# Moving the value-cache loads of a decode-attention kernel from SyncE's DMA queue to ScalarE's

## The chip, the cores and the metric

The kernel runs on one core of one Trainium2 chip. The metric is the device time of one execution in microseconds (us), median of several executions. The profile's span, also quoted, is of one execution and comes out about 2 us shorter. "Tile" always means one unit of the kernel's main loop: one batch row and four heads, with 4 MB of keys, called K(t), and 4 MB of values, V(t); t runs from 0 to 63.

## The reference, cut to what matters

```python
def reference(A_x, A_k_cache, A_v_cache, A_wq, A_wo, B_x, B_w1, B_b1, B_w2, B_b2):
    # 8 batch rows, one query each; 32 heads; 4096 cached positions; head size 128; bf16
    x = A_x
    xn = _layernorm(x, axis=-1)
    # attention: q = xn @ wq; scores = q . k_cache * Dh**-0.5; p = softmax; o = p @ v_cache; o @ wo
    # mlp: gelu(layernorm(xn) @ w1 + b1) @ w2 + b2
    return x + _A_ref(xn, A_k_cache, A_v_cache, A_wq, A_wo) + _B_ref(xn, B_w1, B_b1, B_w2, B_b2)
```

Each cached key and value is used once. The two caches are 537 MB of the 552 MB that are read.

## The kernel before

The program is a list of operations. Each has an engine and a position; every engine runs its operations in order of position, and a small scheduler derives the semaphore waits from the tiles that an operation reads and writes. There are two buffers for keys (`NK = 2`) and two for values (`NV = 2`). All large loads are issued by SyncE ("sp"), in order, on one DMA queue:

```python
def ld(pos, dst, src, W, sem, R=()):
    add("sp", pos, lambda e: e.dma_start(dst, src() if callable(src) else src), R=R, W=W, sem=sem)
...
for t in range(T):                                       # T = 64 tiles
    pos = (-100.0, -98.0)[t] if t < NK else t - 1.5      # K(t): needs K(t-2)'s buffer
    for n, (j0, j1) in enumerate(kpieces(t)):
        ld(pos + 0.01 * n, kview(t)[:, j0:j1, :], ...)
    pos = (0.45, 1.2)[t] if t < NV else t + 0.6          # V(t): needs V(t-2)'s buffer
    for n, (j0, j1) in enumerate(vpieces(t)):            # one piece; V(63) in three
        ld(pos + 0.01 * n, vview(t)[:, j0:j1, :], ...)
...
for hg in range(NG - 1):                                 # output weights, once per 8 tiles, 640 KB
    ld(hg * B + 3.65, wo_sb[:, :, :], ...)
```

So from K(4) on, SyncE issues K(4), V(2), K(5), V(3), ... : K(t+2), then V(t). The work on a tile is this (the line numbers are those of the profile):

- VectorE multiplies three quarters of the keys by the query and sums, in two halves (L549 multiply, L553 add, L556 reduce). It holds the key buffer until the second multiply ends.
- TensorE transposes the other quarter, the first of the tile (L517), ScalarE evicts it, and TensorE multiplies it with the query (L527).
- For two tiles at a time (the last two one by one), the softmax: VectorE's row maximum (L568), transposes on TensorE (L570, L578), ScalarE's exponentials (L588).
- TensorE multiplies the probabilities with the values (L621; L631 for the last piece), about two tiles later: the value product of tile t stands in TensorE's order after the key work of tile t+2. ScalarE evicts it (L640).
- At the end a few multiplications by zero (L784) stand between the last products; they are meant to keep TensorE's clock up.

Of the kernel before, what the change touches and what calls it, by code (L numbers as in the profile page):

```python
# [19 lines left out]
class _Sched:  # L20
# [13 lines left out]
    def add(self, eng, pos, fn, R=(), W=(), X=(), sem=None, sig=False):  # L34
        o = _Op()
        o.pos, o.seq, o.eng, o.fn, o.R, o.W, o.X, o.sem = pos, len(self.ops), eng, fn, R, W, X, sem
        o.sig = sig
        self.ops.append(o)
# [165 lines left out]
def bass_parallel_sum__gqa_block_cached__mixer_channel_mlp__decode_kernel(  # L204
# [16 lines left out]
    HT = 4  # L221
# [3 lines left out]
    T = NG * B  # L225
# [12 lines left out]
    NK, NV, NS = 2, 2, 4  # L238
# [6 lines left out]
    with ExitStack() as es:  # L245
# [6 lines left out]
        wo_sb = sb("wo_sb", [P, HT, D], BF)  # L252
# [65 lines left out]
        add = sch.add  # L318
        TRR = _Ring("TR", 2)

        def kview(t):
            return KV_sb[:, t % NK, :].rearrange("p (j d) -> p j d", d=P)

        def vview(t):
            return KV_sb[:, NK + t % NV, :].rearrange("p (j d) -> p j d", d=P)
# [5 lines left out]
        def tile_src(cache, t):  # L331
            return cache[t % B, span(t // B, HT)].rearrange("h k d -> (h k) d").rearrange("(p j) d -> p j d", p=P)
# [19 lines left out]
        def dve_const2(e):  # L352
# [9 lines left out]
            W=["identneg", "onesb", "sel", "oTn", "wo"] + [(s, i) for s in ("Pt", "rs") for i in range(GT)])  # L362


        def ld(pos, dst, src, W, sem, R=()):
            add("sp", pos, lambda e: e.dma_start(dst, src() if callable(src) else src), R=R, W=W, sem=sem)  # L366

        add("act", -100, lambda e: e.dma_start(x_sb[:, :], x2[:, :]), W=["x"], sem="x")
        add("act", -99.9, lambda e: e.dma_start(b2_sb[:, :], B_b2.partition_broadcast(B)), W=["b2"], sem="b2")
        add("act", -99.8, lambda e: e.dma_start(b1_sb, B_b1.rearrange("(o f) -> o f", o=1)), W=["b1"], sem="b1")  # L370

        ld(-99.0, wq_sb, A_wq.rearrange("(k c) n -> k c n", c=DC), ["wq"], "wq")

        def pvpos(i):
            return 2.0 + i

        def kpieces(t):
            return [(0, NJ)]

        def vpieces(t):  # L380
            return [(0, 64), (64, 96), (96, NJ)] if t == T - 1 else [(0, NJ)]

        for t in range(T):
            pos = (-100.0, -98.0)[t] if t < NK else t - 1.5
            for n, (j0, j1) in enumerate(kpieces(t)):
                ld(pos + 0.01 * n, kview(t)[:, j0:j1, :], lambda t=t, j0=j0, j1=j1: tile_src(A_k_cache, t)[:, j0:j1, :],
                   [("K", t % NK, q) for q in range(j0 // 16, j1 // 16)], "k%d_%d" % (t % NK, n))
            pos = (0.45, 1.2)[t] if t < NV else t + 0.6
            R = (["wqfree"], ["wqfree", "w1free", "hfree"])[t] if t < NV else []
            for n, (j0, j1) in enumerate(vpieces(t)):  # L390
                ld(pos + 0.01 * n, vview(t)[:, j0:j1, :], lambda t=t, j0=j0, j1=j1: tile_src(A_v_cache, t)[:, j0:j1, :],
                   [("V", t % NV, q) for q in range(j0 // 16, j1 // 16)], "v%d_%d" % (t % NV, n), R)
        ld(-95.2, w1_sb, B_w1.rearrange("(k c) f -> k c f", c=DC), ["w1"], "w1")
        ld(-95.1, w2_sb[:, 0:FC, :], B_w2[0:FC * P, :].rearrange("(k c) n -> k c n", c=FC), ["w2"], "w2")
        ld(-95.0, w2_sb[0:FR, FC, :], B_w2[FC * P:F, :], ["w2r"], "w2r")
# [3 lines left out]
               "wo")  # L399

        wo_last = A_wo[(H - HT) * P:H * P, :].rearrange("(a p) n -> p a n", p=P)
        ld(T - 0.1, wo_sb[:, 0:HT - 1, :], wo_last[:, 0:HT - 1, :], ["wo"], "wo")
        ld(T - 0.09, wo_sb[:, HT - 1, :], wo_last[:, HT - 1, :], ["wo3"], "wo3")


        def layernorm(n, pos, src, src_res, dst, dst_res):
# [21 lines left out]
        def transposed(w, pos, src, src_res):  # L428
# [16 lines left out]
            R=["x", "b2"], W=["xb2"])  # L445
# [254 lines left out]
        def pe_zero(e):  # L700
# [6 lines left out]
            R=["zeros"], W=["ACC"], X=["ACC"])  # L707
# [14 lines left out]
        def pe_hidden(e):  # L722
# [10 lines left out]
            R=[it_h], W=["h"], X=[it_h])  # L733

        def pe_hidden_t(e):
# [7 lines left out]
            R=[it_t], W=["hT"], X=[it_t])  # L743

        def pe_mlp2(e):
# [11 lines left out]
            R=["mlp", "xb2"], W=["xb2"], X=[("PVb", 0), ("PVb", 1)])  # L757
# [6 lines left out]
            R=["ACC"], W=["resT"], X=["ACC"])  # L764
# [21 lines left out]
        for pos, n in ((pvpos(T - 2) + 0.25, 2), (pvpos(T - 1) + 0.075, 4), (pvpos(T - 1) + 0.115, 3), (pvpos(T - 1) + 0.2, 1)):  # L786
# [3 lines left out]
            R=["fin"], W=["out0"], X=[("TR", 0)])  # L790
        add("act", END + 2, lambda e: e.activation(out_sb[:, w:D], TRF[32:32 + B, 0, 0:w], ACT.Copy),
            R=["fin"], W=["out1"], X=[("TR", 0, "act")])
# [51 lines left out]
```

## Time and profile before

| | |
|---|---|
| time | 1290.62 us, median of 3 (1290.62 to 1290.68) |
| span of the profiled execution | 1288.9 us |
| DMA engines busy | 99.9% with one queue |
| VectorE busy | 87% |
| TensorE busy, ScalarE busy | 50%, 39% |

The page's list of engines, its rows by slice for VectorE and DMA (busy share in tenths, 40 slices), its list of DMA queues (packets, MB, share of 16 engines), two lines of its costliest groups (busy us, mean ns of one; idle before, what ended it) and two of its DMA issues (count, KB each, median us from issue to landing):

```profile
PE 644.0 (50%) x7931; PEld 408.5 (32%) x7934; DVE 1121.8 (87%) x584; ACT 497.2 (39%) x1243; POOL 0.2 (0%) x4
DVE  4989999898898898898988988988889888889885
DMA  9999999999999999999999999999999999999998
...
q1 hardware_dynamic: 23488, 551.80, 99.9%
...
L549 DVE TENSOR_TENSOR Y_sb<-KV_sb,qbc_sb 128x6144 bf16<-128x6144 bf16 x128 | 429.1, 3353 | 89.3 <-DMA KV_sb<-in_A_k_cache_dram 74.9
...
L621 PE MATMUL PV_ps<-KV_sb,P_sb 128*16 128x512 bf16 x2040 | 225.0, 620 | 139.9 <-DMA KV_sb<-in_A_v_cache_dram 139.7
...
KV_sb<-in_A_k_cache_dram SPq DMA_DIRECT2D x64, 4096.0 KB, 26.8
KV_sb<-in_A_v_cache_dram SPq DMA_DIRECT2D x63, 4096.0 KB, 35.2
```

The DMA engines never rest. A load of 4 MB takes 9.7 us at 431 GB/s but lands 27 or 35 us after its issue: it stands in a queue that always holds two to four tiles. TensorE and VectorE wait for loads, not the other way round.

The end of the chain of waits (start us, duration, what), from the table of pieces in order of time:

```profile
1229.42 35.19 DMA KV_sb<-in_A_v_cache_dram
1264.61 0.04 issue
1264.65 3.34 PE PV_ps L621 x32
1268.00 0.02 issue
1268.01 16.20 DMA KV_sb<-in_A_v_cache_dram
1284.21 0.04 issue
1284.25 0.72 PE PV_ps L631 x32
```

The end is a chain of value loads. V(61) lands at 1264.6 us, its product frees a buffer, V(63) is issued at 1268.0, lands at 1284.2, and 4.7 us later the program is over.

The table of windows (us, then busy time of each engine, the granted TensorE clock, the DMA share and GB/s):

```profile
200.00:1200.00 1000.00, 495.82 (x6077) 316.76 (x6075) 883.82 (x435) 387.77 (x976) 0.00 (x0) 0.54 1.00 431
1270.00:1280.00 10.00, 6.36 (x74) 2.41 (x72) 2.76 (x5) 2.73 (x10) 0.00 (x0) 0.83 0.97 409
1280.00:1285.00 5.00, 3.74 (x60) 1.29 (x52) 0.00 (x0) 0.60 (x2) 0.00 (x0) 1.00 0.85 333
```

431 GB/s in mid-run; VectorE is the third number. And one line of the timeline, VectorE's start on the last tile, K(63):

```profile
1254.93 3.36 DVE L549 TENSOR_TENSOR Y_sb<-KV_sb,qbc_sb 128x6144 bf16<-128x6144 bf16 x1 [1.39 <-DMA KV_sb<-in_A_k_cache_dram]
```

It starts 34.0 us before the end of the span.

### The profile page before, as it was taken

The numbers are of one execution on the slowest core, as the hardware profiler recorded it, in microseconds if no ns is written. First come the engines' busy times: TensorE is split into PE (matmuls) and PEld (weight loads), VectorE is DVE, ScalarE is ACT, GpSimd is POOL, SyncE is SP. The second block draws the span as 40 slices with busy tenths as digits, with TensorE's granted clock in tenths as the row PEclk, the third lists the DMA queues.
The fourth block names the chain that finished last, engine by engine and source line by source line (L and its number), as shares of the span: only waits on it lengthen the run. The fifth ranks groups of instructions, "written<-read, shape, count | busy, mean of one in ns | idle before, by whom it ended". The sixth has DMA issues, their size and how long they took to land.

```text
span 1288.9 us, 19855 instructions
## 1 busy us (share of the span) xinstructions
PE 644.0 (50%) x7931; PEld 408.5 (32%) x7934; DVE 1121.8 (87%) x584; ACT 497.2 (39%) x1243; POOL 0.2 (0%) x4
## 2 busy tenths in 40 slices
PE   2654455454454455454445444444544554455456
PEld 1433233233333233233233232232332332333332
DVE  4989999898898898898988988988889888889885
ACT  1444344334344234343243442443432443423432
POOL 0000000000000000000000000000000000000000
PEclk9955555555655555555555555656556555555557
DMA  9999999999999999999999999999999999999998
GB/s 408 424 426 427 435 427 438 427 428 434 429 433 431 429 431 432 430 433 429 428 436 428 434 427 430 432 432 432 427 431 431 434 429 429 434 429 432 431 431 358
DMA packets 23536, 552.00 MB, mean 428 GB/s; under 512 B 2313, under 2 KB 6497, under 8 KB 6498
## 3 DMA queue, kind: packets, MB, share of 16 engines
q1 hardware_dynamic: 23488, 551.80, 99.9%
q8 instruction: 8, 0.13, 0.0%
q14 instruction: 6, 0.05, 0.0%
q10 hardware_dynamic: 34, 0.02, 0.0%
HBM read 551.80 MB, written 0.01 MB: 428 GB/s over the span
## 4 chain that ended last, share of the span: by engine, by line
DMA 80%; DVE 9%; PE 8%; issue 3%; ACT 0%; SPq 0%; DVEq 0%
DMA KV_sb<-in_A_v_cache_dram 76%; PE PV_ps L621 7%; DVE Y_sb L549 5%; DMA KV_sb<-in_A_k_cache_dram 2%; DVE Y_sb L553 2%; DMA KV_sb<-in_A_wq_dram 2%; DVE S_sb L556 2%; DVE M_sb L568 0%; SPq L366 0%; PE CH_ps L570 0%; PE TR_ps L675 0%; PE PV_ps L631 0%; PE TR_ps L461 0%; DVE rinv_sb L602 0%; DVEq L178 0%
## 5 line engine op out<-in xcount | busy, mean ns | idle before, releaser
L549 DVE TENSOR_TENSOR Y_sb<-KV_sb,qbc_sb 128x6144 bf16<-128x6144 bf16 x128 | 429.1, 3353 | 89.3 <-DMA KV_sb<-in_A_k_cache_dram 74.9
L556 DVE TENSOR_REDUCE S_sb<-Y_sb 128x48 f32<-128x3072 bf16 x128 | 429.2, 3353 | 4.4
L520 ACT ACTIVATE KT_sb<-TR_ps 128x1024 bf16<-128x1024 bf16 x256 | 254.6, 1020 | 228.5 <-PE TR_ps L517 227.0
L621 PE MATMUL PV_ps<-KV_sb,P_sb 128*16 128x512 bf16 x2040 | 225.0, 620 | 139.9 <-DMA KV_sb<-in_A_v_cache_dram 139.7
L517 PE MATMUL TR_ps<-ident_bf,KV_sb 128*128 128x128 bf16 x2048 | 250.2, 310 | 73.7 <-DMA KV_sb<-in_A_k_cache_dram 73.7
L553 DVE TENSOR_TENSOR Y_sb<-Y_sb 128x3072 bf16<-128x3072 bf16 x128 | 225.0, 1758 | 4.4
L517 PEld LDWEIGHTS TR_ps<-ident_bf,KV_sb 128*128 128x128 bf16 x2048 | 202.0, 142 | 84.3 <-DMA KV_sb<-in_A_k_cache_dram 78.3
L527 PE MATMUL S_ps<-qk_sb,KT_sb 128*128 128x4 bf16 x2048 | 98.2, 170 | 136.2 <-ACT KT_sb L520 134.3
L640 ACT ACTIVATE E_sb<-PV_ps 128x512 bf16<-128x512 f32 (+1 forms) x65 | 38.5, 593 | 319.1 <-PE PV_ps L621 317.1
L621 PEld LDWEIGHTS PV_ps<-KV_sb,P_sb 128*16 128x16 bf16 x2040 | 63.3, 124 | 251.8 <-DMA KV_sb<-in_A_v_cache_dram 145.2
L527 PEld LDWEIGHTS S_ps<-qk_sb,KT_sb 128*128 128x128 bf16 x2048 | 86.4, 109 | 167.4 <-ACT KT_sb L520 167.4
L588 ACT ACTIVATE P_sb<-S_sb,NB_sb 32x128 bf16<-32x128 f32 x256 | 101.9, 398 | 3.8
L646 PE MATMUL C_ps<-sel_bf,E_sb 128*128 128x4 bf16 x256 | 17.0, 172 | 135.1 <-DVE rinv_sb L602 113.2
L582 ACT ACTIVATE NB_sb<-CH_ps 128x2 f32<-128x2 f32 (+1 forms) x33 | 5.7, 172 | 171.4 <-PE CH_ps L578 171.4
L570 PE MATMUL CH_ps<-ident_f,M_sb 128*2 128x128 f32 (+1 forms) x33 | 12.1, 366 | 116.3 <-DVE M_sb L568 116.3
L646 PEld LDWEIGHTS C_ps<-sel_bf,E_sb 128*128 128x128 bf16 x256 | 11.5, 104 | 165.0 <-DVE rinv_sb L602 112.6
L537 ACT ACTIVATE S_sb<-S_ps 32x32 f32<-32x32 f32 x256 | 48.3, 189 | 32.2 <-PE S_ps L527 29.9
L588 ACT ACTIVATION_READ_ACCUMULATOR P_sb<-S_sb,NB_sb 32x1 f32 x256 | 47.0, 184 | 0.0
L570 PEld LDWEIGHTS CH_ps<-ident_f,M_sb 128*2 128x2 f32 (+1 forms) x33 | 2.7, 80 | 119.2 <-DVE M_sb L568 119.2
L664 DVE MEMSET oTn_sb<- 128x16 uint32 x30 | 2.2, 72 | 31.1 <-PE ACC_ps L688 31.1
L572 DVE TENSOR_REDUCE M_sb<-CH_ps 2x4 f32<-2x128 f32 (+1 forms) x33 | 9.2, 279 | 15.1 <-PE CH_ps L570 15.1
L599 PEld LDWEIGHTS C_ps<-rs_sb,ones_f 128*128 128x128 f32 x64 | 14.0, 274 | 25.4 <-issue 22.0
(96 smaller groups left out, 201.9 us busy)
## 6 DMA issues: line engine op xcount, KB each, us to landing
KV_sb<-in_A_k_cache_dram SPq DMA_DIRECT2D x64, 4096.0 KB, 26.8
KV_sb<-in_A_v_cache_dram SPq DMA_DIRECT2D x63, 4096.0 KB, 35.2
KV_sb<-in_A_wq_dram SPq DMA_DIRECT2D x1, 5120.0 KB, 23.8
wo_sb<-in_A_wo_dram SPq DMA_DIRECT2D x7, 640.0 KB, 30.9
KV_sb<-in_B_w_dram SPq DMA_DIRECT2D x1, 2160.0 KB, 39.1
w_sb<-in_B_w_dram SPq DMA_DIRECT2D x1, 2080.0 KB, 44.1
KV_sb<-in_A_v_cache_dram SPq DMA_DIRECT2D x1, 2048.0 KB, 12.6
KV_sb<-in_A_v_cache_dram SPq DMA_DIRECT2D x2, 1024.0 KB, 15.2
```

The costliest lines, as they stand in the source:

```text
L517: r = e.transpose(TR_ps[:, it.box[0], jj * P:(jj + 1) * P], kv[:, n * BK + jj, :], ident_bf[:, :])
L520: add("act", t - 0.59 + 0.12 * n, lambda e: e.activation(KT_sb[:, m % NS, :, :].rearrange("p a b -> p (a b)"), TR_ps[:, it.box[0], :], ACT ...
L527: r = e.matmul(S_ps[:, c:c + HT], KT_sb[:, m % NS, jj, :], qk_sb[:, :, i], start=True, stop=True)
L537: r = e.activation(S_sb[s, g % SR, i, 0:JP], S_ps[s, 0:JP * HT].rearrange("p (j a) -> p j a", a=HT)[:, :, a], ACT.Copy)
L549: return e.tensor_tensor(y, kv[:, j0:j1, :], qbc_sb[:, g % 2, i, :][:, None, :].to_broadcast([P, nj, P]), ALU.mult)
L553: lambda e, y=y, y2=y2: e.tensor_tensor(y2, y[:, :, 0:P // 2], y[:, :, P // 2:P], ALU.add),
L556: lambda e, y2=y2, j0=j0, j1=j1: e.tensor_reduce(S_sb[:, g % SR, i, j0:j1], y2, AX.X, ALU.add),
L570: add("pe", c - 0.715, lambda e: e.transpose(M1T_ps[0:n, :], M1_sb[:, 0:n], ident_f[:, :]), R=["M1", "identf"], W=["M1T"], X=["CH"])
L588: r = e.activation(P_sb[s, i, :, a, :], S_sb[s, g % SR, i, :].rearrange("p (m c) -> p m c", c=4), ACT.Exp, bias=NB_sb[s, g % 2, i:i + 1], ...
L621: r = e.matmul(PV_ps[32 * ct:32 * ct + HT * 4, t % 2, :], P_sb[:, i, m, :, :].rearrange("p a c -> p (a c)"), vv[:, 4 * m:4 * m + 4, :].rea ...
L640: add("act", pos, lambda e: e.activation(E_sb[:, k, 0:n], PV_ps[:, k, 0:n], ACT.Copy), R=[("PV", k)] + ["wo"] * (t % GT and not last), W=[ ...
L646: r = e.matmul(OT_i, E_sb[:, t % 2, c * P:(c + 1) * P], sel_bf[:, c:HT * 4:4], start=(c == 0), stop=(c == 3 and not last))
```

## The change

The intent is to give the two streams a queue each, so that SyncE does not hold a key load behind its wait for a value buffer or the reverse, and the issues are shared between two engines. V(0) and V(1) stay on SyncE. No byte and no computation changes.

```diff
-        def ld(pos, dst, src, W, sem, R=()):
-            add("sp", pos, lambda e: e.dma_start(dst, src() if callable(src) else src), R=R, W=W, sem=sem)
+        def ld(pos, dst, src, W, sem, R=(), eng="sp"):
+            add(eng, pos, lambda e: e.dma_start(dst, src() if callable(src) else src), R=R, W=W, sem=sem)
...
-            pos = (0.45, 1.2)[t] if t < NV else t + 0.6
+            pos = (0.45, 1.2)[t] if t < NV else t + 0.225
...
-                   [("V", t % NV, q) for q in range(j0 // 16, j1 // 16)], "v%d_%d" % (t % NV, n), R)
+                   [("V", t % NV, q) for q in range(j0 // 16, j1 // 16)], "v%d_%d" % (t % NV, n), R, "sp" if t < NV else "act")
...
-        ld(T - 0.1, wo_sb[:, 0:HT - 1, :], wo_last[:, 0:HT - 1, :], ["wo"], "wo")
-        ld(T - 0.09, wo_sb[:, HT - 1, :], wo_last[:, HT - 1, :], ["wo3"], "wo3")
+        ld(T - 0.74, wo_sb[:, 0:HT - 1, :], wo_last[:, 0:HT - 1, :], ["wo"], "wo", eng="act")
+        ld(T - 0.73, wo_sb[:, HT - 1, :], wo_last[:, HT - 1, :], ["wo3"], "wo3", eng="act")
```

## The prediction

> **What bounds the kernel now.** The DMA engines. The page's queue list gives the single SyncE queue 99.9% of 16 engines' span, 551.8 MB at 428 GB/s; the table of windows gives 430 to 432 GB/s from 100 to 1250 us. In the DMA records a 32 KB packet takes 1.21 to 1.22 us (433 GB/s on 16 engines) with almost no gap. The chain of waits is 76% V-cache loads. VectorE, next, is 87% busy: per tile 2 x (3.35 + 1.76 + 3.35) = 16.9 us, about 17.5 us with softmax pieces, against 19.4 us for one K and one V load of 4 MB (9.7 us each).
>
> **What the change does.** No byte and no computation is added or removed. V(2) to V(63) and the last output weights are issued by ScalarE, each behind the eviction of a value product (0.60 us), so some 0.6 us later than now; an issue costs about 0.33 us, 64 x 0.33 = 21 us on a ScalarE that is 39% busy. SyncE's issues no longer wait for value products. None of this is on the critical path: loads are issued 27 us (K) and 35 us (V) before they land, so the queue always holds two to four tiles. The Trainium skill ("DMA: Bandwidth & Descriptors", section "Issuing engines are not separate DMA queues") says that issuing from several engines only saves sequencer time; this trace has no idle transfer time to win. Ceiling of the gain: 433/431, under 1%.
>
> **What can get worse: order.** One queue is served first in, first out: K(t+2), then V(t), the order of need; K(63) lands about 30 us before the last V. With two queues each engine alternates by packet (same page, section "Queues, rings and completion order"). The trace agrees: at the start a 1280-byte packet of ScalarE's queue and its semaphore packet stand one 32 KB packet (1.2 to 1.3 us) apart. So:
> 1. K and V transfers overlap; each takes up to 19 us instead of 9.7. Two buffers still cover that: VectorE holds a K buffer 12 us (19.4 + 12 < 38.9), so the engines stay fed.
> 2. A weight load (640 KB, 32 packets of 1280 bytes per engine) alternates with 32 KB value packets and holds back the keys behind it by up to about 10 us, seven times. VectorE has 1.9 us of slack per tile; values run ahead meanwhile. I estimate 0 to 2 us of DMA idle each, 3 us in all.
> 3. Keys lose their lead, and K(63) lands only 15 to 20 us of transfer before the end. After it come VectorE's 17 us, softmax 4 us, the last value product 3.6 us and about 4 us of output: 29 us. Estimate: 3 to 12 us longer tail.
>
> **Prediction.** 1298 us (+0.6%), 80% range 1287 to 1316. Faster by over 2%: 0.03; within 2%: 0.85; slower by over 2%: 0.12.
>
> **What would show it.** Two queues with about half of the bytes each, together 99 to 100% busy until shortly before the end, still about 431 GB/s in mid-run. Keys waiting longer around the weight loads: VectorE idle several us once per 8 tiles. In the last 40 us: DMA below full, VectorE's last tile nearer to the end, the chain passing through VectorE and softmax instead of V loads alone. ScalarE's busy time unchanged.
>
> **What would make it wrong.** If two rings in flight change an engine's rate (1.21 us per 32 KB), every tile scales with it: 1% is 12 us. If arbitration is by bytes, step 2 vanishes and the time is 1290. If keys and values, waiting on each other through TensorE's order, empty both queues once per tile, the change is slower by over 2%.

## The result

| | before | after |
|---|---|---|
| time, median | 1290.65 us (1290.62 to 1290.80, 4 runs) | 1299.66 us (1298.56 to 1300.22, 4 runs) |
| span of the profiled execution | 1288.9 us | 1297.8 us |
| ratio | | 1.0068, 95% interval 1.0053 to 1.0084 |

The change costs 9.0 us, 0.7%.

The lines of the page and of the table of windows for the kernel after, in the same order as those of before:

```profile
PE 627.5 (48%) x7931; PEld 402.8 (31%) x7934; DVE 1120.2 (86%) x584; ACT 497.5 (38%) x1243; POOL 0.2 (0%) x4
DVE  4979799987999979998799878999699887998895
DMA  9999999999999999999999999999999999999996
...
q1 hardware_dynamic: 13728, 291.09, 52.4%
q10 hardware_dynamic: 9794, 260.73, 46.8%
...
L549 DVE TENSOR_TENSOR Y_sb<-KV_sb,qbc_sb 128x6144 bf16<-128x6144 bf16 x128 | 428.5, 3348 | 102.8 <-DMA KV_sb<-in_A_k_cache_dram 88.3
...
L621 PE MATMUL PV_ps<-KV_sb,P_sb 128*16 128x512 bf16 x2040 | 216.1, 598 | 0.0
...
KV_sb<-in_A_k_cache_dram SPq DMA_DIRECT2D x64, 4096.0 KB, 26.3
KV_sb<-in_A_v_cache_dram ACTq DMA_DIRECT2D x61, 4096.0 KB, 23.9
```

```profile
200.00:1200.00 1000.00, 479.42 (x6093) 312.40 (x6089) 881.96 (x433) 387.38 (x962) 0.00 (x0) 0.56 1.00 431
1270.00:1280.00 10.00, 9.26 (x80) 3.72 (x78) 9.90 (x5) 3.49 (x8) 0.00 (x0) 0.50 0.61 238
1280.00:1285.00 5.00, 1.85 (x16) 0.89 (x19) 4.43 (x5) 0.00 (x0) 0.00 (x0) 0.50 0.98 418
```

Two queues carry about half each, and together they are as full as one was: 431 GB/s in mid-run. The product with the values now waits for no value load at all (0.0 us, before 139.7): values come early. VectorE waits longer for keys (88.3 us, before 74.9), and not evenly: its row by slices dips to 7 or 6 about once in five slices, which is once per output-weight load. But those dips lie in a stretch where the DMA engines are full, so they need not cost time. What differs visibly in the DMA rate is the end: from 1270 to 1280 us the engines are only 61% busy, and VectorE is busy throughout. The end of the chain of waits (lines left out between):

```profile
1239.80 27.00 DMA KV_sb<-in_A_k_cache_dram
1266.81 0.02 issue
1266.83 3.37 DVE Y_sb L549
...
1280.47 3.37 DVE S_sb L556
1283.83 0.02 issue
1283.86 0.30 DVE M_sb L568
...
1285.22 3.28 PE PV_ps L621 x31
...
1289.66 0.97 PE PV_ps L621 x16
...
1293.34 0.65 PE PV_ps L631 x32
```

The chain no longer runs through value loads. K(63) is awaited until 1266.8 us; then come VectorE's two halves (17.0 us, to 1283.9), the softmax, the products of V(62) and V(63), and the output, 31.0 us in all to 1297.8. VectorE starts K(63) 11.9 us later than before (1254.93). Before there were 34.0 us from that start to the end, 3.0 us more than this computation needs; 11.9 - 3.0 = 8.9 us is the whole difference of the spans.

Why does K(63) come later? From the DMA records one can count when the last packet of each tile has moved, and take the lead of the keys as the landing of V(t) minus that of K(t+2):

```
tile t           4      8     11     12     14     16     20     24     28     36     44     52     56     61
before         9.7    9.8   10.3    9.7    9.7    9.7    9.7    9.7    9.7    9.7    9.7    9.7    9.7    9.7
after         -4.0    1.2    1.0  -15.8   -4.9    1.2  -15.9    1.2  -15.9  -15.8  -15.3  -16.0   -1.2   -1.2
```

Before, the queue is first in, first out, and keys land one load (9.7 us) ahead. After, K(t+2) and V(t) land within one 32 KB packet (1.2 us) of each other, except after each weight load (t = 12, 20, 28, ...), where the keys fall 16 us behind and recover in four tiles. So at the end V(61), V(62) and V(63) follow K(63) before; after, V(61) is there already.

This table counts packets. What an engine waits for is the semaphore of a load, which goes up in sixteen steps (512 are recorded for the 32 loads into one key buffer); the last step is the landing (VectorE starts K(63) within 0.02 us of it in both kernels). Read so, the leads of the table are the same in kind: 9.7 to 10.0 us before; after, about 0 when undisturbed and -16 to -17 us at a weight load. K(63) lands at 1254.9 us before and at 1266.8 after, V(62) at 1274.3 and 1275.6. So V(62) follows K(63) by 19.4 us before and by 8.8 us after, which is 10.6 us of the 11.9. The other 1.3 us is transfer time lost over the run, by which V(62) comes later. With 9.7 us for V(63), about 18.5 us of transfer follow K(63) in the changed kernel.

### The profile page after: what moved, and what is told of

Its sections match the earlier page's. It is cut to its first block, busy times and chain, and to the rows that moved or that the text cites. A ratio compares the mean times of both kernels' runs of the same rounds, so it can differ in the third digit from the quotient of the medians.

```text
span 1297.8 us, 19843 instructions
## 1 busy us (share of the span) xinstructions
PE 627.5 (48%) x7931; PEld 402.8 (31%) x7934; DVE 1120.2 (86%) x584; ACT 497.5 (38%) x1243; POOL 0.2 (0%) x4
## 4 chain that ended last, share of the span: by engine, by line
DMA 43%; DVE 36%; issue 13%; PE 4%; ACT 3%; DVEq 0%; SPq 0%; ACTq 0%
DMA KV_sb<-in_A_k_cache_dram 41%; DVE Y_sb L549 21%; DVE Y_sb L553 9%; DVE S_sb L556 5%; PE PV_ps L621 2%; DMA KV_sb<-in_A_wq_dram 2%; ACT P_sb L588 2%; ACT KT_sb L520 1%; PE TR_ps L517 1%; DVE M_sb L568 0%; PE S_ps L527 0%; PE CH_ps L570 0%; DVE rinv_sb L602 0%; DVE M_sb L572 0%; PE CH_ps L578 0%
## 5 line engine op out<-in xcount | busy, mean ns | idle before, releaser
L549 DVE TENSOR_TENSOR Y_sb<-KV_sb,qbc_sb 128x6144 bf16<-128x6144 bf16 x128 | 428.5, 3348 | 102.8 <-DMA KV_sb<-in_A_k_cache_dram 88.3
L517 PE MATMUL TR_ps<-ident_bf,KV_sb 128*128 128x128 bf16 x2048 | 248.2, 308 | 88.3 <-DMA KV_sb<-in_A_k_cache_dram 88.3
L621 PE MATMUL PV_ps<-KV_sb,P_sb 128*16 128x512 bf16 x2040 | 216.1, 598 | 0.0
L537 ACT ACTIVATE S_sb<-S_ps 32x32 f32<-32x32 f32 x256 | 48.3, 189 | 32.1 <-PE S_ps L527 29.8
L664 DVE MEMSET oTn_sb<- 128x16 uint32 x30 | 2.2, 72 | 31.1 <-PE ACC_ps L688 31.1
L688 PE MATMUL ACC_ps<-oTn_sb,wo_sb 128*128 128x8 bf16 x600 | 20.8, 169 | 0.0
## 6 DMA issues: line engine op xcount, KB each, us to landing
wo_sb<-in_A_wo_dram SPq DMA_DIRECT2D x7, 640.0 KB, 30.9
```

What stands on the lines that cost most here:

```text
L517: r = e.transpose(TR_ps[:, it.box[0], jj * P:(jj + 1) * P], kv[:, n * BK + jj, :], ident_bf[:, :])
L537: r = e.activation(S_sb[s, g % SR, i, 0:JP], S_ps[s, 0:JP * HT].rearrange("p (j a) -> p j a", a=HT)[:, :, a], ACT.Copy)
L549: return e.tensor_tensor(y, kv[:, j0:j1, :], qbc_sb[:, g % 2, i, :][:, None, :].to_broadcast([P, nj, P]), ALU.mult)
L621: r = e.matmul(PV_ps[32 * ct:32 * ct + HT * 4, t % 2, :], P_sb[:, i, m, :, :].rearrange("p a c -> p (a c)"), vv[:, 4 * m:4 * m + 4, :].rea ...
L688: r = e.matmul(ACC_ps[:, c * B:(c + 1) * B], wo_sb[:, a, c * P:(c + 1) * P], oTn_sb[:, a, :], start=False, stop=False, skip_group_check=True)
```

## The experiments

The theory (A): the engines serve the two queues by turns, the keys lose the lead that the order of one queue gave them, and the loss is the computation after K(63), which comes too late. Rivals: (B) two queues in flight cost every tile a little; (C) the weight loads, held back by values, cost DMA time seven times or are what takes the lead away.

The kernel's loops wait for semaphores against a register. The experiments wait against constants only, so all twelve, controls included, have the loops of all engines written out (`emit_rolled(...)` becomes `emit(...)`). They are to be compared with the written-out controls, each through the kernel before of its own rounds. Every interval of a ratio is about 0.0016 to either side, 2 us; the repeats of one kernel differ by under 2 us.

### Controls

> Control: the kernel before with its loops written out, so that every wait is against a constant; nothing else differs. Every theory expects the kernel before's time, 1290.6 us, within 3 us, keys landing 9.7 us ahead of the values two tiles behind them, and about 431 GB/s in mid-run.

> Control: the changed kernel with its loops written out. Every theory expects its time, 1299 us, within 3 us, the lead of the keys falling to about -16 us at each weight load and recovering to about 0, K(63) landing about 12 us later than in the kernel before, and 3 us of idle DMA before the last value load.

Measured: 1301.63 us (ratio to the kernel before 1.0084) and 1308.49 us (1.0136). Both expectations missed in the absolute: writing out the loops costs 11.0 and 8.8 us. The loss from the change is 6.9 us here. The instruction queue carries 62 packets and 1.02 MB instead of 8 and 0.13 MB, and in the last 30 us of the control of before only about six tenths of the engine time is used for several us, so some engines were behind others. By the steps of its semaphore, K(63) took 12.6 us from the first to the last in the control of before (2.3 us in the kernel before) and 3.2 us in the control of after (1.8 us in the kernel after). So the one-queue control has a delay of its own at its end. The 9.0 us between the original kernels are the cleaner measure of the loss, and a difference of 2 or 3 us between written-out runs says little. That the instruction traffic is the cause is argued, not tested. The rest is as in the originals: keys lead by 9.7 us in one, and in the other fall after weight loads to -6 to -15 us and recover to within 2.3 us of zero; VectorE starts K(63) at 1264.96 and 1275.86 us. In the chains of waits the control of before ends with a value load, that of after with K(63):

```profile
1278.26 16.06 DMA KV_sb<-in_A_v_cache_dram
```

```profile
1248.84 27.00 DMA KV_sb<-in_A_k_cache_dram
...
1275.86 3.37 DVE Y_sb L549
```

### Only the last six value loads back on SyncE

```diff
-  ..., R, "sp" if t < NV else "act")
+  ..., R, "act" if NV <= t < T - 6 else "sp")
-  pos = ... t + 0.225
+  pos = ... t + (0.225 if t < T - 6 else 0.6)     # and the last weights back on SyncE
```

> The changed kernel written out, but the last six value loads, V(58) to V(63), and the last weights go back to SyncE; 56 value loads stay on ScalarE. Theory A (the loss is the tail: keys lose their lead over the values, and K(63) lands too late for the work that follows it): 1290 to 1293 us, K(63) again about 10 us ahead of V(61). Rival B (two rings in flight cost every tile a little): 1297 to 1300 us, as 56 of 62 loads are still shared. Rival C (the weight loads held back by values cost DMA time seven times): 1296 to 1300 us.

Measured: 1304.36 us (1.0106). Relative to the controls 2.7 us over the one-queue kernel and 4.1 under the two-queue one. (Counted from 1290.6 us, which was expected for the control, theory A allowed 0 to 2 us over it, the rivals 5 to 9.) The lead is back at 9.7 us at t = 61, and most of the loss is gone, though 56 loads still share. But VectorE had not caught up with its work: it started K(63) only at 1270.84, about 6 us after K(63) had landed (1265.1 by its semaphore; the 7 us of the next expectation count from its last packet, 1263.8). The next run asks whether the rest is that backlog.

### The last fourteen back on SyncE

The same edit with `T - 14`, which takes in the last of the seven weight loads.

> As the run that put the last six values back on SyncE (1304.4 us), now the last fourteen, V(50) to V(63), with the last of the seven weight loads. In that run VectorE still had a backlog from the last weight load and began K(63) 7 us after it landed. Theory A with this backlog: 1301.5 to 1303 us, K(63) begun when it lands or soon after. If the 2.7 us left there are a cost of the shared part: 1303.5 to 1304.5 us.

Measured: 1301.66 us (1.0082), the same as the one-queue control (1301.63). The chain of this run ends in value loads again, and VectorE starts K(63) when it lands. From the chain and the timeline:

```profile
1241.24 35.15 DMA KV_sb<-in_A_v_cache_dram
...
1280.08 15.97 DMA KV_sb<-in_A_v_cache_dram
```

```profile
1266.71 3.36 DVE L549 TENSOR_TENSOR Y_sb<-KV_sb,qbc_sb 128x6144 bf16<-128x6144 bf16 x1 [1.36 <-DMA KV_sb<-in_A_k_cache_dram]
```

With 48 value loads on the second queue the time is that of one queue. That does not prove that they are free: the rate from 200 to 1200 us is 428 GB/s here and 430 in the one-queue control, and K(63) starts 1.8 us later; the control loses about as much at its uneven end. But the loss of the change as a whole does not come from them. Rival B is out as the main cause.

### Only the last six value loads on ScalarE

```diff
-  ..., R, "sp" if t < NV else "act")
+  ..., R, "sp" if t < T - 6 else "act")           # positions accordingly
```

> The opposite: the kernel before written out, but only V(58) to V(63) and the last weights go to ScalarE. No weight load falls in the shared part. Theory A (tail): 1296 to 1301 us, nearly the whole loss from six loads. Rival B (every tile): 1291 to 1292 us. Rival C (weights): 1290 to 1291 us.

Measured: 1310.35 us (1.0149), 8.7 us over the one-queue control and slower even than the full change written out. The lead is 9.7 us up to t = 56 and -3.9 at t = 61. Six loads on an empty second queue overtake keys that wait on the first, and VectorE starts K(63) at 1277.76 us. No weight load falls in that stretch. Rivals B and C cannot give this. From the chain of waits:

```profile
1250.38 27.36 DMA KV_sb<-in_A_k_cache_dram
...
1277.76 3.37 DVE Y_sb L549
```

### One queue, values first

```diff
-  pos = (0.45, 1.2)[t] if t < NV else t + 0.6     # kernel before: behind K(t+2), at t + 0.5
+  pos = (0.45, 1.2)[t] if t < NV else t + 0.225   # ahead of K(t+2); still SyncE
```

> The kernel before written out (1301.6 us), everything on SyncE's one queue, but each value load V(t) is put ahead of the key load K(t+2) in SyncE's order instead of behind it. If the order of landing is what costs (theory A), one queue alone loses as two do: keys land about 10 us behind the values, K(63) about 20 us before the end of the transfers, and 1307 to 1318 us. If two rings in flight are needed for the loss, 1301 to 1303 us.

Measured: 1307.98 us (1.0134), 6.4 us over the control and equal to the change (1.0136) within the interval. The lead is -9.7 us throughout. The chain of waits ends as that of the change does:

```profile
1247.57 27.23 DMA KV_sb<-in_A_k_cache_dram
1274.80 0.02 issue
1274.83 3.37 DVE Y_sb L549
...
1291.84 0.30 DVE M_sb L568
```

A second queue is not needed for the loss. The order of landing is enough. From 200 to 1200 us this one queue moves 427.7 MB of loads, by the DMA records; the one-queue control moves 428.9 and the two-queue control 426.9. So more than half of the small drop in rate needs no second queue either.

### The weight loads on ScalarE

```diff
-  "wo")
+  "wo", eng="act")       # the seven weight loads, hg * B + 3.65
```

> The changed kernel written out (1308.5 us), but the seven weight loads go to ScalarE's queue, behind the values. Theory A with arbitration by packet: now the values and not the keys stand behind the weights, so each weight load moves the keys ahead by 10 us or more, the dips of the lead to -16 us are gone, VectorE's idle before keys shrinks, and K(63) lands ahead of V(61) as long as nothing takes the lead away again: 1301 to 1304 us. If sharing alone drives the lead back to about 0 without any weight load in the way, K(63) and V(61) land together and the time stays 1307 to 1309 us; then my step 2 is not the cause of step 3.

Measured: 1306.81 us (1.0125), 1.7 us under the control, within the interval. The first expectation missed, the second is nearer. The dips are gone and are humps now: the lead rises to 6 us after the first weight load and to 14 to 19 us after the others. But it falls back, to 1.7 us at t = 24 and 0.6 at t = 61. TensorE now waits 152 us for values (in the full change 0.0). K(63) starts at 1273.60.

### No weight loads at all

```diff
-  for hg in range(NG - 1):
+  for hg in ():          # wrong result on purpose
```

> The changed kernel written out without the seven weight loads (wrong result on purpose; 4.6 MB less, worth 10.6 us at 431 GB/s). The lead must show no dips to -16 us. If weight loads cause the lost lead: lead near +9 us at the end, and 1308.5 - 10.6 - 6 to 7 = about 1291 us. If sharing alone settles the lead at about 0: K(63) with V(61), the same tail as in the changed kernel, and about 1298 us.

> Control for the run without weights (1295.5 us with two queues): the kernel before written out, without the seven weight loads (wrong result on purpose). By bytes 1301.6 - 10.6 = 1291 us. The difference to 1295.5 us is what sharing alone costs; what is missing to the 6.9 us between the two written-out kernels is the weights' part. My guess: sharing 4 to 5 us, weights 2 to 3 us.

Measured: with two queues 1295.48 us (1.0036), with one 1288.41 us (0.9982), a difference of 7.1 us. With the weight loads it is 6.9. So no part of the weights is seen (each difference is uncertain by 2 to 3 us), and sharing alone gives a loss of this size; my guess of 2 to 3 us for the weights missed. The lead without weights is between -1.7 and 1.8 us from t = 4 on:

```
tile t           4      8     11     12     14     16     20     24     28     36     44     52     56     61
two queues     1.2    1.2    1.1    1.1    1.1    0.5   -0.9   -1.0   -1.1   -0.9   -1.2   -0.9   -1.0   -1.7
one queue      9.9    9.8    9.7    9.7    9.8    9.7    9.9    9.8    9.7    9.8    9.7    9.7    9.7    9.7
```

The lead is lost at the start, when V(2) is issued on an empty second queue instead of standing behind K(3) and K(4). After that, equal turns keep K(t+2) and V(t) side by side. Rival C is out as the main cause.

The one-queue control gained 13.2 us from losing the weights; by bytes (4.6 MB at 431 GB/s) I had expected 10.6. The DMA records explain it: the 3584 packets of 1280 bytes take 13.1 us of all 16 engines.

### Packets of half the size

```diff
   def vpieces(t):                                  # and, in the other run, kpieces(t)
-      return ... [(0, NJ)]
+      return ... [(0, NJ // 2), (NJ // 2, NJ)]     # two loads, each half of every row: 16 KB packets
```

> The changed kernel written out (1308.5 us), each value load cut into two of half a row, so that a value packet is 16 KB and a key packet still 32 KB. If the engines alternate by packet, keys get two thirds of the rate while both wait, values one third: the lead rises well above 0 and the time falls to 1301 to 1304 us. If they alternate by bytes, the lead at the end stays about 0 and the time 1307 to 1310 us.

> The same with the key loads cut in two: key packets of 16 KB, value packets of 32 KB. By packet: keys get one third while both wait, the lead falls to -8 to -16 us, values wait for their turn with full buffers, K(63) lands last but V(63), and the time rises to 1312 to 1322 us. By bytes: 1307 to 1310 us.

Measured: half-size value packets 1307.37 us (1.0126), half-size key packets 1316.96 us (1.0201). The leads:

```
tile t           4      8     11     12     14     16     20     24     28     36     44     52     56     61
half values  -12.1   16.3   13.7   -1.0   16.2   19.3    7.6   19.2    5.2    6.2    4.8    5.5   17.7    9.6
half keys     -3.0  -12.2   -1.8   -2.2   -3.8  -10.0   -2.1   -9.2   -0.4   -8.0    0.0   -1.9   -7.6   -8.3
```

The queue with the larger packets gets ahead, in both directions, so the engines take turns by packet and not by byte. The records of the changed kernel show the turns directly: from 500 to 560 us, with each packet put behind the one that ended where it starts (the records do not name the engine), 736 of 778 key and value packets follow one of the other queue. The time of the second run is as expected. That of the first missed: the lead is 9.6 us at the end, yet only 1.1 us is won. VectorE starts K(63) at 1274.87, because by then it is late for another reason: values are too late now. TensorE waits 218 us for them, and the row maximum on VectorE stands behind TensorE (54 us of VectorE's waits for that transpose, 15 in the full change). A larger lead of the keys is no gain either.

### The product of tile 62 moved ahead

```diff
-  p0 = pvpos(t)
+  p0 = pvpos(t) - (0.858 if t == T - 2 else 0.0)
```

> The changed kernel written out (1308.5 us), with one thing moved: TensorE does the value product of tile 62 ahead of the softmax transposes of tile 63, so it no longer stands behind VectorE's last tile. If the tail is the computation after K(63), this takes about 3.4 us off: 1304 to 1306 us. If the tail is the transfers, whose last value load is late by its own wait, 1308 to 1309 us.

Measured: 1309.72 us (1.0147), 1.2 us over the control: missed. The product itself moved as intended, to before 1291.7 us, but its eviction on ScalarE stands in ScalarE's order behind the exponentials of tile 63. The last part of that product and its eviction in the timeline, then the chain of this run:

```profile
1291.23 0.39 PE L621 MATMUL PV_ps<-KV_sb,P_sb 128*16 128x512 bf16 x4
1296.80 0.60 ACT L640 ACTIVATE E_sb<-PV_ps 128x512 bf16<-128x512 f32 x1
```

```profile
1293.31 0.30 DVE M_sb L568
...
1296.31 0.49 ACT P_sb L588 x2
1296.79 0.01 issue
1296.80 0.60 ACT E_sb L640
```

My edit moved the work from TensorE's in-order queue to ScalarE's. With both moved, part of the tail might be won; that was not run. The end still follows VectorE's start on K(63): 1276.29 us, plus 32.1.

### All runs by one number

| run | VectorE starts K(63) | span | from there to the end |
|---|---|---|---|
| before | 1254.93 | 1288.9 | 34.0 |
| after | 1266.83 | 1297.8 | 31.0 |
| control, one queue | 1264.96 | 1299.8 | 34.8 |
| control, two queues | 1275.86 | 1307.1 | 31.2 |
| last six back | 1270.84 | 1301.9 | 31.1 |
| last fourteen back | 1266.71 | 1300.7 | 34.0 |
| only last six moved | 1277.76 | 1308.8 | 31.0 |
| one queue, values first | 1274.83 | 1305.7 | 30.9 |
| weights on ScalarE | 1273.60 | 1304.9 | 31.3 |
| no weights, two queues | 1262.22 | 1294.1 | 31.9 |
| no weights, one queue | 1252.58 | 1286.4 | 33.8 |
| half value packets | 1274.87 | 1306.1 | 31.2 |
| half key packets | 1284.24 | 1316.4 | 32.2 |
| product 62 first | 1276.29 | 1308.4 | 32.1 |

Where the last keys come late enough, the end is 31 to 32 us after VectorE starts them. Where it is about 34 us or more, the last value load decides, as in the chain of the kernel before. No kernel run here beats the kernel before; the only shorter time (1288.41 us) is of the run that leaves out loads and gives a wrong result.

## Why the prediction was right

The time was predicted as 1298 us (+0.6%) and came out at 1299.66 (+0.7%).

- *The DMA engines bound the kernel, and there is nothing to win*: right. The rate is 431 GB/s in mid-run in both.
- *Turns by packet*: right. Both runs with half-size packets show it.
- *Step 1, the engines stay fed with two buffers each*: right; in mid-run the DMA share is 1.00 in both.
- *Step 2, weight loads hold the keys back and cost about 3 us*: half right, and not the cause of the loss. The delays are there, seven times, and longer than I said: the lead falls by 17 us, not 10. They do not take the lead away for good. Without any weight load the lead is as small and the loss is 7.1 instead of 6.9 us. The cause is the first turn: a value load on an empty queue overtakes the keys that wait on the other. V(62) lands 1.3 us late, less than the 3 us I gave, and what part of it the weights have was not separated in the original kernels.
- *Step 3, the tail*: right in kind and size. I expected 15 to 20 us of transfer after K(63), 29 us of computation and 3 to 12 us of loss; measured were 18.5, 31.0 and 7.6 of the 8.9 us. The prediction puts this down to the turns between the queues, and that holds: the lead goes without any weight load. The total came closer than its parts: the lost transfer was smaller than the 3 us I gave (1.3), the computation 2 us longer than I said, and the range for the tail was wide (3 to 12 us). That 1298 missed by only 1.7 us is in part luck.
- *DMA below full in the last 40 us*: right, 61% from 1270 to 1280 us. It is a symptom. V(63) is issued late because its buffer waits for a product that stands behind the key work of tile 63, but the chain does not pass through V(63).
- *ScalarE's busy time unchanged*: right, 497.5 against 497.2 us.

What stays open: why the lead comes back to nearly 0 after every dip or hump and not to another value (that one queue runs empty in between fits, but was not tested); and why writing out the loops costs 9 to 11 us.

## What to carry to other kernels

When the DMA engines are full all the time, as here, a second queue brings no bandwidth (431 GB/s with one and with two), but it replaces the order in which you issued the loads by turns between the queues; if that order was the order of need, you lose it. Judge it at the end of the run: what matters is how much computation follows the last load of each kind, and the load with the longest work behind it should land first. Turns go by packet, so the stream with the longer rows gets more (the lead at the end was 9.6 us with half-size value packets and -8.3 with half-size key packets, against 0.0), and a load of short rows holds up whatever stands behind it on its queue (the keys fell back by 17 us at a weight load).

## What the Trainium skill lacked or had wrong

- "DMA: Bandwidth & Descriptors", section "Issuing engines are not separate DMA queues", says that issuing from several engines only saves sequencer time. For bandwidth this agrees (431 GB/s with one queue and with two). It says that the loads interleave, but not that the order of landing can cost time: keys 9.7 us ahead became keys level with values, and that cost most of the 9.0 us.
- The same page, section "Queues, rings and completion order", has turns by packet, with about 9 to 17 descriptors in a typical packet. Here a turn was one row of 32 KB: a 1280-byte packet and its semaphore packet stood 1.2 to 1.3 us apart, the time of one such row, and halving the rows of one stream moved the lead by up to about 20 us in favour of the other. The page does not say that the longer rows get the larger share.
- The same page, section "Specifications", gives 512 bytes as the least transfer for line rate. Packets of 1280 bytes took 58 ns in the mean, 22 GB/s of an engine, against 1219 ns and 26.9 GB/s for 32 KB; leaving out 4.6 MB of them saved 13.2 us instead of 10.6.
- "Runtime: NRT & Kernel Launch", section "Terms", has the instruction memory of an engine refilled in blocks of 16 KiB; the written-out controls agree (62 packets and 1.02 MB on the instruction queue, against 8 and 0.13 MB). The page has no figure for what such traffic costs where the DMA engines are full; its section "Instruction fetch mechanics" calls the cost mostly hidden. With the loops written out the time rose by 8.8 and 11.0 us, but that the traffic is the cause was not tested.
